# Sliding-window attention into an expert layer: five more of the stream's sums sessions in the turned form

## The chip, the cores and the metric

The kernel runs on one core of one Trainium2 chip. The metric is the device time of one execution in microseconds (us). Before the change three runs gave 301.45, 302.57 and 302.14 us; the median is 302.14 us.

## The reference

Attention with a window of 32 keys to each side, 8 batches of 8 heads, 576 positions, head width 64; then the heads side by side are the rows of x, 4608 tokens of 512, which go through a two-layer network with a SMELU between the layers.

```python
def _attn_ref(q, k, v):                      # 8, 8, 576, 64
    scores = scale * np.matmul(q, k.transpose(0, 1, 3, 2))
    mask = np.abs(pos[:, None] - pos[None, :]) <= 32
    scores = np.where(mask, scores, -1000000000.0)
    attn = np.exp(scores - np.max(scores, axis=-1, keepdims=True))
    attn = attn / (np.sum(attn, axis=-1, keepdims=True) + 1e-09)
    return np.matmul(attn, v)

def _moe_ref(x, w_in, w_out):                # 4608x512, 512x2048, 2048x512
    h = x @ w_in
    g = np.where(h >= 1, h, np.where(h <= -1, 0.0, (h + 1) ** 2 / 4))
    return g @ w_out
```

## The kernel before

Everything is in bf16 with f32 sums in PSUM, and one core does two kinds of work interleaved by hand: the attention, which makes x, and the two products of the network, which use it.

**Positions.** The main loop counts positions `a`. At each position it issues one projection `hp`: up to position 71 one token tile of 256 tokens and 256 of the 2048 hidden columns (line 653, eight matmuls), so eight positions to a tile; from 72 to 135 ("wide") 512 tokens and 128 columns (line 674, four matmuls), so sixteen positions to 512 tokens. The wide part begins with token 2304: positions 72 to 87 use tokens 2304 to 2815, positions 88 to 103 tokens 2816 to 3327. After the projection come its elementwise steps (line 692 on ScalarE, lines 698 and 700 on VectorE), then the attention work written down for this position, then a given number of matmuls of the second product (`op`, line 607 or 625), whose results leave through `osb` by a DMA on the sync engine's queue SP (line 615). PE takes its instructions in exactly this order.

**Sessions.** Batches 1 to 7 are one stream of 63 chunks of 64 keys. It is handled in turns, numbered from 0; from turn 5 on a turn has three chunks. At a position of the list below one turn's sums are made and the next turn's scores are begun; this is called session `k` here after the turn whose sums it makes.

```python
sl = [26.0, 29, 33, 36, 41, 45, 49, 53, 59, 66, 71, 74, 81, 87, 95, 99, 108, 111, 123]   # sessions 4, 5, 6, ...
```

So sessions 9 to 14 stand at positions 45, 49, 53, 59, 66 and 71. Session `k` (from 5 on) makes x for the 192 tokens that begin at 1120 + 192(k - 5): session 11 for 2272 to 2463, session 13 for 2656 to 2847, session 16 for 3232 to 3423. Hence positions 72 to 87 need session 13's x, and positions 88 to 103 session 16's. Position 64, the first of tile 8 (tokens 2048 to 2303), needs all of session 10's and the first 32 tokens of session 11's.

**Two forms of a session.** `stream_scores` (lines 282 to 294) makes the scores of a turn, their exponential `wt` and the band mask. Then:

- The plain form (`stream_sums`, line 410): v is the stationary side, 32 small matmuls; a column of ones against `rows` (the pairwise sum of two halves of `wt`, made by VectorE in lines 301 to 305) gives the denominators in 8 more matmuls; ScalarE turns them into reciprocals by Ln and Exp (lines 319 to 323); VectorE multiplies into `xT` (line 327), where x lies already the way the projection reads it.
- The turned form (`turned_sums`, line 346): `wt` is the stationary side and v with a column of ones moves, 48 small matmuls; the queries are then on the partitions and the denominator is one more column. VectorE makes the reciprocals (line 354) and two products into a tile `xn` (line 358); DMA transposes issued on SP (lines 364 and 367) write `xT`. `xn` has two buffers.

**Loads and the SP queue.** From batch 3 on, q and k of a batch come by GpSimd's DMA queue (POOL, line 106) into `qn` and `kn`, with v behind (line 116); each of the two has one buffer, so the loads of the next batch wait for the transposes of this one (a small copy on POOL, line 716, marks that). Once `qn` has landed, SP issues one DMA transpose `qT<-qn` (line 196), and one `kT<-kn` likewise; they stand in SP's order at positions 46 and 48 for batch 5, at 65 and 69 for batch 6, at 89 and 91 for batch 7. SP takes its instructions in order: one that waits holds all that stand behind it.

```python
xps: for b, positions in [[23, 24], [33, 34], [46, 48], [65, 69], [89, 91]]   # qT, kT of batches 3 to 7
```

Of the kernel before, what the change touches and what calls it, by code (L numbers as in the profile page):

```python
# [14 lines left out]
def kernel(  # L15
# [33 lines left out]
    LATE = 5  # L49
    SPLIT = range(20, 25)  # L50
    EARLY = 3, 4
    TURNED = range(14, 23)

    const = ctx.enter_context(tc.tile_pool(name="const", bufs=1))
    nat = ctx.enter_context(tc.tile_pool(name="nat", bufs=2))
# [208 lines left out]
    def stream_scores(k, eng, pool=ps_s):  # L264
# [30 lines left out]
        M = turn_of(k)  # L295
        if k in TURNED:
            return
# [9 lines left out]
    def turn_of(k):  # L307

        return next(m for s, e, m in STREAMS if s == turns[k][0])
# [61 lines left out]
    def stream_sums(k, pool=ps_n):  # L371

        if k in TURNED:
            return turned_sums(k, pool)
# [374 lines left out]
```

## Time and profile before

| | before |
|---|---|
| median of three runs | 302.14 us |
| the profiled execution | 301.69 us |
| its span, first to last instruction | 299.9 us |
| PE busy | 288.4 us, 96% |
| VectorE (DVE) busy | 230.3 us, 77% |
| ScalarE (ACT) busy | 188.9 us, 63% |
| DMA queue of POOL (q0), share of 16 engines | 91.6% |
| DMA queue of SP (q1), share of 16 engines | 30.3% |

The profile shows one execution. Times are microseconds from the start of the span. A row of a timeline gives start, duration, engine, source line, operation, output and input tiles and a count; an engine name with a q is that engine's instruction queue, where a DMA's duration is the time to issue it, not to finish it. "To landing" is the time from the issue to the data's arrival. Idle time of an engine that is not on the path costs nothing.

### The profile page before, as it was taken

The numbers are of one execution on the slowest core, as the hardware profiler recorded it, in microseconds if no ns is written. First come the engines' busy times: TensorE is split into PE (matmuls) and PEld (weight loads), VectorE is DVE, ScalarE is ACT, GpSimd is POOL, SyncE is SP. The second block draws the span as 40 slices with busy tenths as digits, with TensorE's granted clock in tenths as the row PEclk, the third lists the DMA queues.
The fourth block names the chain that finished last, engine by engine and source line by source line (L and its number), as shares of the span: only waits on it lengthen the run. The fifth ranks groups of instructions, "written<-read, shape, count | busy, mean of one in ns | idle before, by whom it ended". The sixth has DMA issues, their size and how long they took to land.

```text
span 299.9 us, 8061 instructions
## 1 busy us (share of the span) xinstructions
PE 288.4 (96%) x3349; PEld 177.9 (59%) x3380; DVE 230.3 (77%) x371; ACT 188.9 (63%) x345; POOL 79.5 (27%) x102
## 2 busy tenths in 40 slices
PE   8789999999999999999999999999999999999995
PEld 4468778876666666677654444444444444456544
DVE  3369887999999999889898889598878887546700
ACT  3678794777777666775875466565467446675301
POOL 8997450072190452091046000031000000000000
PEclk9999999999999999999999999999999999999999
DMA  9999999999999999999989971589212212100121
GB/s 153 182 189 201 179 189 156 180 160 146 183 161 136 198 192 158 197 140 158 136 124 123 179 91 42 113 148 135 65 35 63 61 37 62 37 35 36 39 103 70
DMA packets 146293, 37.45 MB, mean 125 GB/s; under 512 B 130129, under 2 KB 142673, under 8 KB 146257
## 3 DMA queue, kind: packets, MB, share of 16 engines
q0 software_dynamic: 103600, 18.06, 91.6%
q1 hardware_dynamic: 42512, 18.59, 30.3%
q8 instruction: 26, 0.43, 0.6%
q10 hardware_dynamic: 144, 0.29, 0.4%
q14 instruction: 11, 0.08, 0.1%
HBM read 36.70 MB, written 9.44 MB: 154 GB/s over the span
## 4 chain that ended last, share of the span: by engine, by line
PE 85%; DVE 4%; ACT 4%; issue 3%; DMA 2%; POOL 1%; POOLq 0%; ACTq 0%; DVEq 0%
PE op L607 35%; PE hp L653 20%; PE hp L674 18%; PE op L625 3%; PE bb L410 2%; DMA vn<-in_v_dram 2%; PE bb L282 2%; PE bb L346 2%; PE op L598 1%; DVE mx L698 1%; ACT rr L692 1%; POOL vn L116 1%; ACT rc L454 1%; PE tp L189 1%; DVE wt L294 1%
## 5 line engine op out<-in xcount | busy, mean ns | idle before, releaser
L692 ACT ACTIVATE rr<-hp 128x512 f32<-128x512 f32 x144 | 85.3, 595 | 80.2 <-PE hp L674 38.5
L607 PE MATMUL op<-w_out,gT 128*128 128x512 bf16 x471 | 120.0, 379 | 3.2 <-issue 3.0
L698 DVE TENSOR_TENSOR mx<-hp,rr 128x512 f32<-128x512 f32 x106 | 72.7, 686 | 16.2 <-ACT rr L692 15.3
L653 PE MATMUL hp<-xT,w_in 128*128 128x256 bf16 x640 | 82.5, 273 | 1.7 <-DMA w_in<-in_moe_w_in_dram 0.6
L700 DVE SCALAR_TENSOR_TENSOR gT<-rr,mx 128x512 bf16<-128x512 f32 x105 | 72.7, 692 | 3.6
L607 PEld LDWEIGHTS <-gT 128*128 128x128 bf16 x496 | 47.0, 98 | 47.6
L653 PEld LDWEIGHTS <-w_in 128*128 128x128 bf16 x640 | 61.5, 98 | 21.3 <-issue 3.2
L674 PE MATMUL hp<-xT,w_in 128*128 128x512 bf16 x252 | 64.5, 379 | 0.2
L674 PEld LDWEIGHTS <-w_in 128*128 128x128 bf16 x256 | 25.0, 98 | 30.3 <-issue 0.2
L696 DVE SCALAR_TENSOR_TENSOR gT<-hp,mx 128x512 bf16<-128x512 f32 x38 | 26.2, 689 | 17.4 <-ACT mx L695 15.3
L116 POOL DMA_DIRECT2D vn<-in_v_dram x32 | 27.6, 879 | 2.1 <-issue 2.1
L695 ACT ACTIVATE mx<-rr 128x512 f32<-128x512 f32 x38 | 23.9, 630 | 1.2
L716 POOL COPY gate<-kT 128x2 bf16<-128x2 bf16 x4 | 1.4, 345 | 87.9 <-DMA kT<-kn 87.9
L288 ACT ACTIVATE wt<-bb 128x1024 bf16<-128x1024 f32 (+2 forms) x23 | 22.1, 966 | 3.6 <-PE bb L282 2.8
L294 DVE TENSOR_TENSOR wt<-wt,band 128x1536 bf16<-128x1536 bf16 (+2 forms) x23 | 20.4, 888 | 4.3 <-ACT wt L291 2.8
L611 ACT COPY osb<-op 128x512 f32<-128x512 f32 x23 | 13.3, 577 | 11.3 <-PE op L607 11.3
L625 PE MATMUL op<-w_out,gT 128*128 128x256 bf16 x128 | 16.3, 273 | 0.0
L106 POOL DMA_DIRECT2D qn<-in_q_dram x12 | 14.8, 1250 | 4.1 <-DMA kT<-kn 3.7
L106 POOL DMA_DIRECT2D kn<-in_k_dram x12 | 14.8, 1260 | 0.2 <-issue 0.2
L625 PEld LDWEIGHTS <-gT 128*128 128x128 bf16 x128 | 12.5, 98 | 1.4
L327 DVE TENSOR_TENSOR xT<-bb,rc 128x768 bf16<-128x768 f32 (+4 forms) x16 | 11.9, 754 | 1.8 <-ACT rc L323 1.7
L291 ACT ACTIVATE wt<-sp 128x256 bf16<-128x256 f32 (+1 forms) x36 | 11.2, 368 | 0.0
(88 smaller groups left out, 198.4 us busy)
## 6 DMA issues: line engine op xcount, KB each, us to landing
out_dram<-osb SPq DMA_DIRECT2D x30, 256.0 KB, 2.7
vn<-in_v_dram POOLq DMA_DIRECT2D x32, 144.0 KB, 5.7
qn<-in_q_dram POOLq DMA_DIRECT2D x12, 288.0 KB, 9.3
kn<-in_k_dram POOLq DMA_DIRECT2D x12, 288.0 KB, 10.8
w_in<-in_moe_w_in_dram POOLq DMA_DIRECT2D x15, 128.0 KB, 4.9
out_dram<-osb SPq DMA_DIRECT2D x12, 128.0 KB, 1.9
w_out<-in_moe_w_out_dram POOLq DMA_DIRECT2D x4, 256.0 KB, 9.5
w_out<-in_moe_w_out_dram POOLq DMA_DIRECT2D x2, 512.0 KB, 12.0
```

What stands on the lines that cost most here:

```text
L106: nc.gpsimd.dma_start(out=x[:, :, h], in_=src[b, NY * h:NY * h + NY].rearrange("y s d -> (y s) d") .rearrange("(u p) d -> p u d", p=128))
L116: nc.gpsimd.dma_start(out=vn[b][64 * a:64 * a + 64, :, h, :D], in_=v[b, y:y + 2].rearrange("y s d -> (y s) d") .rearrange("(c r) d -> r c ...
L294: V.tensor_mul(x, x, band[:, :128].rearrange("p (m n j) -> p m n j", m=1, n=1).to_broadcast(list(x.shape)))
L607: nc.tensor.matmul(op[tt], gT[:, j, home(tt // 2), 128 * (tt % 2):128 * (tt % 2) + 128], w_out[:, j], start=j == 0, stop=j == 15)
L625: nc.tensor.matmul(o[:, tt], gT[:, j, p, 128 * tt:128 * tt + 128], w_out[:, j, 256 * half:256 * half + 256], start=not done, stop=len(done ...
L653: nc.tensor.matmul(hp[:, j], w_in[:, kk, 256 * f + 128 * j:256 * f + 128 * j + 128], xT[:, kk, r0:r0 + TB], start=first and n == 0, stop=l ...
L674: nc.tensor.matmul(hp.rearrange("p n t -> p (n t)"), w_in[:, kk, 128 * f:128 * f + 128], xT[:, kk, r0:r0 + 2 * TB], start=n == 0, stop=n == 3)
L692: A.activation(rr, hp, AF.Relu, scale=0.5, bias=0.5)
L695: A.activation(mx, rr, AF.Square)
L696: V.scalar_tensor_tensor(g, hp, 1.0, mx, op0=ALU.max, op1=ALU.min)
L698: V.tensor_max(mx, hp, rr)
L700: V.scalar_tensor_tensor(g, rr, 1.0, mx, op0=ALU.min, op1=ALU.mult)
```

## The change

One constant: which sessions use the turned form.

```diff
-    TURNED = range(14, 23)
+    TURNED = range(9, 23)
```

Sessions 9, 10, 11, 12 and 13 go from `stream_sums` to `turned_sums`; positions, loads, pools and everything else stay. The function that they call now, shortened (its end, `scale`, is queued for VectorE at the next position):

```python
    def turned_sums(k, pool=ps_n):
        bb = two_banks(pool)
        s, m, lo, hi = ranges[k]
        ...
        for part in (todo[:8], todo[8:]):
            for back in (1, 0):
                for g, e, n, y, h in part:
                    ...
                    for a in range(2):
                        nc.tensor.matmul(bb[HD[e], a, E * n:E * n + E], wt[HD[a], 2 * h + y, j:j + 64],
                                         vn[1 + c // NC][HD[a], NC * y + c % NC, h, :E],
                                         start=(a, e) not in seen, stop=True, skip_group_check=True)
        def scale():
            V.reciprocal(rs, x[:, :, :, D])
            xn = early.tile([128, 2, S], BF, name="xn", tag="kh", bufs=2).rearrange("p h s -> p (h s)")
            ...
                V.tensor_mul(p.rearrange("p (a n d) -> p a n d", a=2, d=D), x[:, :, n0:n1, :D],
                             rs[:, :, n0:n1].rearrange("p a (n e) -> p a n e", e=1).to_broadcast([128, 2, n1 - n0, D]))
            t0 = (S + lo) % RING
            cuts = (32, 64) if RING - t0 == 32 else ()
            for p0, p1 in zip((0, *cuts), (*cuts, 128)):
                r0 = (t0 + p0) % RING
                nc.sync.dma_start_transpose(out=xT[:, :, r0:r0 + p1 - p0], in_=parts[0][p0:p1])
            r0 = (t0 + 128) % RING
            for y in range(2):
                nc.sync.dma_start_transpose(out=xT[:, y::2, r0:r0 + 64], in_=parts[1][HD[y]])
```

In the built program, SP's order around the new transposes becomes (those of lines 364 and 367 are "x"; an output is one transfer of line 615): two outputs, **x of 9**, an output, qT and kT of batch 5, **x of 10**, an output, **x of 11** (five DMAs, since its tokens cross the end of the ring that `xT` is), two outputs, **x of 12**, an output, qT of batch 6, **x of 13**, an output, kT of batch 6, x of 14, and so on as before. Each of the other four has three DMAs, so 17 are added.

## The prediction

> **What bounds the kernel now.** I read the page first: busy times, then the chain that ended last, then the queues and DMA issues.
>
> ```profile
> span 299.9 us, 8061 instructions
> PE 288.4 (96%) x3349; PEld 177.9 (59%) x3380; DVE 230.3 (77%) x371; ACT 188.9 (63%) x345; POOL 79.5 (27%) x102
> ...
> DMA  9999999999999999999989971589212212100121
> ...
> PE 85%; DVE 4%; ACT 4%; issue 3%; DMA 2%; POOL 1%; POOLq 0%; ACTq 0%; DVEq 0%
> ...
> xT<-xn SPq DMA_TRANSPOSE x27, 3.4
> ```
>
> PE is the bound: 85% of the chain is PE's. PE works in program order, so the time changes only through PE work removed or through a wait put in front of a PE instruction. The DMA row says where a wait could come from: the engines are full until slice 20 (about 150 us), and sessions 9 to 13 lie inside that; of those turned so far only 14 and 15 meet such load.
>
> Next the stretch of the five sessions, in the sums by windows (PE, PEld, DVE, ACT, POOL busy):
>
> ```profile
> 102.00:112.00 10.00, 9.81 (x183) 7.04 (x184) 9.52 (x15) 6.86 (x15) 6.20 (x7) 1.00 1.49 189
> ...
> sum 60.00, PE 58.94 PEld 41.12 DVE 53.88 ACT 42.50 POOL 17.47; mean PE 9.82 PEld 6.85 DVE 8.98 ACT 7.08 POOL 2.91
> ```
>
> From 92 to 152 us PE is idle for 60.00 - 58.94 = 1.06 us. No relief of another engine can gain more than that here.
>
> **The PE work of a session.** PE's timeline: sessions 9, 12 and 13 (plain, L410), 14 and 15 (turned, L346), the projections of positions 56 and 64 (L653, counted on from the sessions, whose positions are known), and the first wide one (L674):
>
> ```profile
> 102.86 0.54 PE L410 MATMUL bb<-wt,vn 64*64 64x64 bf16 x32
> ...
> 124.96 1.04 PE L653 MATMUL hp<-xT,w_in 128*128 128x256 bf16 x8
> ...
> 130.49 0.54 PE L410 MATMUL bb<-wt,vn 64*64 64x64 bf16 x32
> ...
> 139.05 1.04 PE L653 MATMUL hp<-xT,w_in 128*128 128x256 bf16 x8
> ...
> 142.62 0.54 PE L410 MATMUL bb<-wt,vn 64*64 64x64 bf16 x32
> ...
> 143.80 1.24 PE L607 MATMUL op<-w_out,gT 128*128 128x512 bf16 x5 [0.16 <-issue]
> ...
> 151.98 0.68 PE L346 MATMUL bb<-vn,wt 64*64 64x65 bf16 x48
> ...
> 153.16 0.81 PE L607 MATMUL op<-w_out,gT 128*128 128x512 bf16 x3 [0.16 <-issue]
> 153.81 1.03 PE L674 MATMUL hp<-xT,w_in 128*128 128x512 bf16 x4
> ...
> 158.86 0.58 PE L346 MATMUL bb<-vn,wt 64*64 64x65 bf16 x48
> ...
> 159.91 0.38 PE L607 MATMUL op<-w_out,gT 128*128 128x512 bf16 x1 [0.16 <-issue]
> ```
>
> From the first small matmul to the next large one: plain (13) 143.80 - 142.62 = 1.18; turned 153.16 - 151.98 = 1.18 and 159.91 - 158.86 = 1.05. So a turned session saves 0 to 0.13 us of PE, the five together 0 to 0.65; I take 0.3, near the middle, as the two turned rows are one at each end.
>
> **VectorE and ScalarE.** VectorE loses the row sums (L301) and the product into xT (L327), and gets a reciprocal (L354) and two products (L358):
>
> ```profile
> L327 DVE TENSOR_TENSOR xT<-bb,rc 128x768 bf16<-128x768 f32 (+4 forms) x16 | 11.9, 754 | 1.8 <-ACT rc L323 1.7
> L358 DVE TENSOR_TENSOR xn<-bb,rs 128x512 bf16<-128x512 f32 (+1 forms) x18 | 9.2, 553 | 0.3
> L301 DVE TENSOR_TENSOR rows<-wt 128x768 bf16<-128x768 bf16 (+1 forms) x11 | 5.6, 510 | 0.4
> L354 DVE RECIPROCAL rs<-bb 128x12 f32<-128x12 f32 x9 | 2.0, 225 | 0.0
> ```
>
> That is 0.754 + 0.510 = 1.26 out, 0.225 + 2 x 0.553 = 1.33 in: nothing. The Ln and Exp on ScalarE go, and with them VectorE's short waits for them. PE hides both: it waits for neither, by the 1.06 us above. I cost them at nothing.
>
> **The DMA transposes, and who waits.** The five sessions add 17 DMAs to SP, on transfers that share the engines with the loads. SP's timeline, then POOL's around the loads of batches 6 and 7:
>
> ```profile
> 117.50 3.78 SPq L196 DMA_TRANSPOSE qT<-qn  x1
> ...
> 142.39 4.41 SPq L196 DMA_TRANSPOSE qT<-qn  x1
> ...
> 148.53 3.26 SPq L196 DMA_TRANSPOSE kT<-kn  x1
> 156.39 1.19 SPq L364 DMA_TRANSPOSE xT<-xn  x1
> 157.67 2.48 SPq L367 DMA_TRANSPOSE xT<-xn  x2
> ```
>
> ```profile
> SPq L196 <- DMA qn<-in_q_dram: 88.9, 7, 47.5
> ```
>
> ```profile
> 127.39 0.73 POOL L716 COPY gate<-kT 128x2 bf16<-128x2 bf16 x1 [13.33 <-DMA kT<-kn]
> ```
>
> The second fence is SP's waits: SP's qT transposes wait for qn, whose loads come behind the batch before's kT through the gate on POOL. It is one serial chain: kT of batch 5, gate, loads of batch 6, qT of batch 6 at 142.39. Before the change only outputs stood behind that wait. Now x of 13 stands right behind qT of batch 6, and x of 10 behind batch 5's; whoever waits for x is PE.
>
> Deadlines: position 72 at 153.81 needs x of 13; position 64 at 139.05 needs x of 10 and the head of x of 11. x of 9 is needed at position 56, 22 us after its session (124.96 - 102.86), and x of 12 at 72, 23 us after (153.81 - 130.49): projections hide both.
>
> How long x takes is in the turned sessions' landings, with loads running (156 to 168 us) and without (205 to 256 us), line 364:
>
> ```profile
> DMA to landing us min/median/max: 6.3/7.1/8.0
> ```
>
> ```profile
> DMA to landing us min/median/max: 2.4/2.4/4.3
> ```
>
> What x costs the loads is in the DMA issues of 128 to 138 us, where no x is on the queue, and of 154 to 164 us, where two sets are:
>
> ```profile
> qn<-in_q_dram POOLq DMA_DIRECT2D x2, 288.0 KB, 9.6
> kn<-in_k_dram POOLq DMA_DIRECT2D x2, 288.0 KB, 11.3
> ```
>
> ```profile
> qn<-in_q_dram POOLq DMA_DIRECT2D x2, 288.0 KB, 9.2
> kn<-in_k_dram POOLq DMA_DIRECT2D x2, 288.0 KB, 14.3
> ```
>
> Two sets make kn land 3.0 us later and qn not at all: 1.5 us a set at the end of the loads, 0 for the part loaded first. The upper bound is the engines' whole time for a set, a third of a qT or kT by bytes, whose landings (line 196, 90 to 160 us) were:
>
> ```profile
> DMA to landing us min/median/max: 4.9/5.9/8.4
> ```
>
> So at most 8.4 / 3 = 2.8 us a set. The Trainium skill, "DMA: Bandwidth & Descriptors", section "Issuing engines are not separate DMA queues", speaks against the change: DMAs of different engines run on the same 16 engines and interleave, so a second queue saves issue time alone. By that rule a set would cost its full engine time, the upper bound; qn's rows say less, kn's half of it.
>
> *Delay of qT of batch 6.* In its chain are x of 9 (during batch 5's loads) and, during batch 6's, x of 10 (its tail), 11 and 12: about 3.5 sets. Bounds 0 and 3.5 x 2.8 = 9.8 us. The chain passes through kn and kT of batch 5, so the 1.5 applies to x of 9; for qn of batch 6 the truth is between 0 and 1.5 a set. I take 1.3 a set, near the upper of these because outputs too now fall into that load: 4.5 us.
>
> *x of 13.* Its first DMA can go when its VectorE work is done, by session 14's delay 142.62 + (156.39 - 151.98) = 147.03, and when SP has issued qT, 142.39 + 4.41 = 146.80: together, with no delay. Plus 4.5 it goes at 151.5; the last of the three starts 2.5 later (157.67 + 1.24 - 156.39) and lands 3.4 after that, the median of all 27 x transposes, between 2.4 and 8.0, nearer the unloaded end because the loads of batch 6 are almost in. That is 157.4, against 153.81: PE waits **3.6 us** in front of position 72. With the bounds: no delay and 2.4 gives 151.95, in time by 1.9; 9.8 and 8.0 gives 167.4, late by 13.5.
>
> *x of 10 and 11.* Batch 5's kT follows its qT (117.50 + 3.78 = 121.3), with x of 9's price of 1.5 to 2.8 at about 123.3; its issue takes some 3.3 us, x of 10's three DMAs 3.7, so the head of 11 goes by about 131, behind an output. Landing in 8.0 it is there at 139.0: just in time for 139.05. A wait here comes off the next one. Cost nothing; if late, it is part of the 3.6.
>
> *What is late next.* kT of batch 6 goes behind x of 13, at 151.5 + 3.7 = 155.2 instead of 148.53, and batch 7's loads, which wait for it, come some 7 us later too. They then meet x of 16:
>
> ```profile
> 176.79 3.57 SPq L367 DMA_TRANSPOSE xT<-xn  x2
> ```
>
> ```profile
> 183.59 1.03 PE L674 MATMUL hp<-xT,w_in 128*128 128x512 bf16 x4
> ```
>
> Its last DMA starts at 176.79 + 3.57 - 1.24 = 179.1 (an issue is 2.48 / 2 = 1.24) and position 88 needs it at 183.59. Landing in 2.4 leaves 2.1 us, in 8.0 it is late by 3.5. Loads reach there only in part; I take 0.5. Later sessions meet no loads. The outputs queued behind have `osb`'s three buffers.
>
> *A wait and the clock.* The granted clock is 1.00 in the windows above. At the very start PE was slow, in its timeline, against the end, in the chain in order of time:
>
> ```profile
> 1.20 4.88 PE L506 MATMUL z<-gT 128*128 128x512 bf16 x11 [1.20 <-DVE gT L138]
> ```
>
> ```profile
> 281.35 5.83 PE op L607 x27
> ```
>
> 4.88 / 11 = 0.44 us a matmul there against 5.83 / 27 = 0.22 later: half speed. If a wait brought that back for as long, it would cost 2.4 us. The Trainium skill, "TensorE: Matmul & The Clock Gate", section "What's actually happening", says an idle window of about 3.4 us does so; by that rule a wait of 3.6 lies at its edge.
>
> **Sum.** 301.69 of the profiled execution (1.8 of it outside the span) - 0.3 + 3.6 + 0.5 = 305.5 us. The median shown is 302.14, 0.45 above that execution, inside its own spread, so I add nothing.
>
> **The rivals.**
>
> *In time: not slower.* The loads give way less than I think. From 154 us on qn landed in 9.2 with two sets beside it, 9.6 without: for it a set cost nothing. If the delay of qT stays under about 0.9 us with 3.4 to land (1.9 with 2.4), x of 13 arrives before 153.81 and only PE's saving is left: 301.69 - 0.3 = 301.4, 301.0 with all of it. Against it: kn's 3.0 us, and x's own 7.1. It decides at that 1 to 2 us of delay.
>
> *Late and cold.* As forecast, and PE comes back at half speed for a stretch: 305.5 + 2.4 = 307.9; with a full-price delay (2 us a set, 7.0 in all, and so 2.5 more) 310.4. For: PE's idle time of 1.06 us in 60 shows no wait of this size, so no row tells what follows one. Against: it needs a wait longer than forecast, or a poor phase.
>
> *Late by both bounds.* The engines give each set its whole time and x lands as under load: over 310, up to 315.
>
> **How the numbers follow.** Late, forecast: 0.55. Late and cold: 0.17. In time or late by under 2 us: 0.23. By both bounds: 0.05. The range goes from the in-time case, 301.3, to late and cold, 310. About 0.5%, 1.5 us either way of 302.14, is what a measurement of this kernel can tell from no change. Faster by that would need 300.6: more than all PE's saving, 0.03. Same: the in-time case and waits of up to 2 us, 0.2. Slower: 0.77. The forecast case's own range is 303.7 to 308.
>
> **What would show it.** Right: PE idle of 2 to 7 us just before the first L674, ended by a DMA `xT<-xn`; qT of batch 6 issued at 145 to 149; L346 x672 in all, and no L319 to L323 from 100 to 150 us; each of the five session stretches 1.05 to 1.18. Cold: PEclk below 9 after that wait. Wrong: qT of batch 6 still near 142.4 and no wait at position 72; or a wait elsewhere, at position 64 or on VectorE for an `xn` buffer, which I hold to be free in time.

## The result, and the profile after

The changed kernel takes 311.97 us (median of six runs, 308.06 to 314.2) against 301.87 of the kernel before (also six): slower by a ratio of 1.0284, 95% interval 1.0253 to 1.0315. Every ratio here leaves out runs that lie over 1.5% above the fastest of the same kernel, of this set 313.93 and 314.2 us, while the medians are of all runs. The profiled execution took 312.66 us, its span is 310.9. A second set of five runs gave 310.31 and a ratio of 1.0269 (1.0247 to 1.0291).

The page of the changed kernel first: span and busy times, the slices of PE, its granted clock and the DMA engines, then two groups.

```profile
span 310.9 us, 8162 instructions
PE 292.8 (94%) x3389; PEld 178.7 (57%) x3420; DVE 229.3 (74%) x374; ACT 181.7 (58%) x325; POOL 80.2 (26%) x102
...
PE   8789999999999999959969999999999999999995
...
PEclk9999999999999999995997999999999999999999
DMA  9999999999999999999997999199311201101021
...
L653 PE MATMUL hp<-xT,w_in 128*128 128x256 bf16 x640 | 84.7, 277 | 5.9 <-DVE mx L698 4.3
...
L358 DVE TENSOR_TENSOR xn<-bb,rs 128x512 bf16<-128x512 f32 (+1 forms) x28 | 14.3, 553 | 5.3 <-DMA xT<-xn 4.8
```

The span grew by 11.0 us, PE's busy time by 4.4 (288.4 to 292.8). PE's row has two dents, the eighteenth and the twenty-first slice, and just behind each the granted clock falls: PE stood still twice and then ran slowly. The group of L358 names a wait that the prediction had ruled out: VectorE waited 4.8 us, once, for a DMA transpose.

PE's timeline of the changed kernel, from session 12 (130.40) on:

```profile
130.40 0.58 PE L346 MATMUL bb<-vn,wt 64*64 64x65 bf16 x48
...
140.39 1.87 PE L653 MATMUL hp<-xT,w_in 128*128 128x256 bf16 x8 [4.02 <-DVE mx L698]
...
149.49 0.58 PE L346 MATMUL bb<-vn,wt 64*64 64x65 bf16 x48
...
158.72 0.68 PE L346 MATMUL bb<-vn,wt 64*64 64x65 bf16 x48
...
163.10 1.61 PE L674 MATMUL hp<-xT,w_in 128*128 128x512 bf16 x4 [2.40 <-DVE xn L358]
```

In square brackets is PE's idle time before the row. Session 8 began at 94.96 (before: 94.65, a difference from the start of the span), session 12 at 130.40 (before: 130.49): three turned sessions (9 to 11) have won 0.40 us, 0.13 each, and nothing is lost yet. Session 13 comes 6.87 us late (142.62 before), session 14 6.74 (151.98 before), session 15 at 169.86 instead of 158.86, 11.0 late; from there the two kernels run alike. So there are two losses: around position 62 6.87 + 0.09 + the 0.13 that session 12 won, 7.1 us, and around position 72 11.0 - 6.74 = 4.3 us. Of the first 4.02 is waiting, of the second 2.40; the rest, 3.1 and 1.9, is slow running. The sums by windows, with the granted clock as third figure from the end, show it:

```profile
120.00:136.00 16.00, 15.69 (x172) 10.58 (x174) 11.89 (x20) 9.80 (x18) 3.59 (x5) 1.00 1.48 144
136.00:140.00 4.00, 0.38 (x2) 0.10 (x1) 1.28 (x3) 0.55 (x2) 4.00 (x5) 0.94 1.96 173
140.00:147.00 7.00, 6.38 (x28) 4.00 (x29) 4.40 (x7) 1.45 (x3) 1.11 (x1) 0.55 2.90 102
147.00:160.00 13.00, 12.68 (x222) 9.13 (x223) 11.00 (x18) 7.70 (x14) 0.00 (x0) 1.00 1.83 175
160.00:164.00 4.00, 1.60 (x6) 0.42 (x5) 3.17 (x6) 1.24 (x3) 0.00 (x0) 0.93 0.29 58
164.00:168.00 4.00, 4.00 (x13) 1.55 (x12) 1.38 (x2) 1.94 (x4) 0.00 (x0) 0.64 1.18 199
```

Behind the first wait the clock is 0.55 over 7 us, behind the second 0.64 over 4; the eight matmuls of one projection at 140.39 took 1.87 us where they take 1.04 at full clock.

What made PE wait is on VectorE's, ScalarE's and SP's timelines of the changed kernel:

```profile
133.69 0.23 DVE L354 RECIPROCAL rs<-bb 128x12 f32<-128x12 f32 x1
138.72 1.02 DVE L358 TENSOR_TENSOR xn<-bb,rs 128x512 bf16<-128x512 f32 x2 [4.81 <-DMA xT<-xn]
```

```profile
139.66 0.59 ACT L611 COPY osb<-op 128x512 f32<-128x512 f32 x1 [3.45 <-DMA out_dram<-osb]
```

```profile
107.39 1.19 SPq L364 DMA_TRANSPOSE xT<-xn  x1
108.67 2.52 SPq L367 DMA_TRANSPOSE xT<-xn  x2
123.11 4.08 SPq L196 DMA_TRANSPOSE qT<-qn  x1
127.35 2.73 SPq L196 DMA_TRANSPOSE kT<-kn  x1
130.19 1.22 SPq L364 DMA_TRANSPOSE xT<-xn  x1
131.51 3.40 SPq L367 DMA_TRANSPOSE xT<-xn  x2
...
151.84 6.39 SPq L196 DMA_TRANSPOSE qT<-qn  x1
158.32 1.22 SPq L364 DMA_TRANSPOSE xT<-xn  x1
159.67 2.88 SPq L367 DMA_TRANSPOSE xT<-xn  x2
```

x of 9 (107.39) runs beside batch 5's loads; qT of batch 5 goes at 123.11 instead of 117.50, and x of 10 behind it only at 130.19. Session 12 needs the `xn` buffer that x of 10 is read from, so VectorE stands still from 133.9 to 138.7 with all its elementwise work behind it, and PE runs out of free `hp` tiles: the first wait. ScalarE stood still until 139.66 as well, for an output that SP issued behind x of 10 (at 135.01); this trace alone does not separate the two. qT of batch 6 then goes at 151.84 instead of 142.39, and x of 13, right behind it, at 158.32: PE waits for it at position 72, the second wait. (The profile names VectorE there, a product for session 14 that ended at 163.0; the second DMA of x of 13 landed then too, 3.3 us after its issue at 159.67, and position 72 needs it.)

The second set's profiled execution of the same kernel (312.38 us) lost about as much, but by other waits. PE's timeline and SP's:

```profile
137.67 1.03 PE L653 MATMUL hp<-xT,w_in 128*128 128x256 bf16 x8 [1.16 <-DVE mx L698]
...
142.00 1.05 PE L653 MATMUL hp<-xT,w_in 128*128 128x256 bf16 x8 [1.53 <-DMA xT<-xn]
...
161.96 1.87 PE L674 MATMUL hp<-xT,w_in 128*128 128x512 bf16 x4 [5.11 <-DMA xT<-xn]
```

```profile
120.65 4.19 SPq L196 DMA_TRANSPOSE qT<-qn  x1
...
147.20 7.51 SPq L196 DMA_TRANSPOSE qT<-qn  x1
154.80 1.23 SPq L364 DMA_TRANSPOSE xT<-xn  x1
```

Here PE waited 7.80 us in all, most of it at position 72, and only the last wait had half speed behind it. qT of batch 6 was less late, but SP took 7.51 us to issue it.

### The profile page after: what moved, and what is told of

Same layout as the page of the kernel before. It is cut to its first block, busy times and chain, and to the rows that moved or that the text cites. A ratio compares the mean times of both kernels' runs of the same rounds, so it can differ in the third digit from the quotient of the medians.

```text
span 310.9 us, 8162 instructions
## 1 busy us (share of the span) xinstructions
PE 292.8 (94%) x3389; PEld 178.7 (57%) x3420; DVE 229.3 (74%) x374; ACT 181.7 (58%) x325; POOL 80.2 (26%) x102
## 5 line engine op out<-in xcount | busy, mean ns | idle before, releaser
L653 PE MATMUL hp<-xT,w_in 128*128 128x256 bf16 x640 | 84.7, 277 | 5.9 <-DVE mx L698 4.3
L653 PEld LDWEIGHTS <-w_in 128*128 128x128 bf16 x640 | 62.4, 99 | 26.9 <-issue 8.4
L674 PE MATMUL hp<-xT,w_in 128*128 128x512 bf16 x252 | 65.8, 385 | 2.6 <-DVE xn L358 2.4
L674 PEld LDWEIGHTS <-w_in 128*128 128x128 bf16 x256 | 25.2, 99 | 33.7 <-issue 4.3
L358 DVE TENSOR_TENSOR xn<-bb,rs 128x512 bf16<-128x512 f32 (+1 forms) x28 | 14.3, 553 | 5.3 <-DMA xT<-xn 4.8
```

Source lines behind the costliest of these rows:

```text
L653: nc.tensor.matmul(hp[:, j], w_in[:, kk, 256 * f + 128 * j:256 * f + 128 * j + 128], xT[:, kk, r0:r0 + TB], start=first and n == 0, stop=l ...
L674: nc.tensor.matmul(hp.rearrange("p n t -> p (n t)"), w_in[:, kk, 128 * f:128 * f + 128], xT[:, kk, r0:r0 + 2 * TB], start=n == 0, stop=n == 3)
```

## The experiments

**Fewer sessions turned.** Two kernels:

```diff
-    TURNED = range(9, 23)
+    TURNED = range(13, 23)     # t13
+    TURNED = range(12, 23)     # t12
```

> One session (13) turned instead of five. Theory, that the time is lost because x of the turned sessions shares the DMA engines with the loads of batches 5 and 6: here x meets next to none of them, qT of batch 6 stays near 142.4 us, x of 13 lands at 152 to 154 us against position 72 at 153.8, and the time is 301.0 to 302.5 us. Rival, that the SP order alone (x of 13 behind qT) costs the second wait: a PE wait of about 2 us stays in front of position 72, 304 us.

> Sessions 12 and 13 turned. Theory (loads and x share the engines): one set beside the loads of batch 6 delays its qT by some 4 to 5 us, x of 13 lands at 156 to 158 us, PE waits 2 to 4 us at position 72: 303.5 to 307 us. Rival (the xn buffers alone): no buffer is short here, 301.5 us.

Session 13 alone: 301.79 us, ratio 0.9999 (0.9985 to 1.0013). Sessions 12 and 13: 303.78 us, ratio 1.0057 (1.0035 to 1.0079). SP's timeline of the first, then of the second:

```profile
142.71 4.32 SPq L196 DMA_TRANSPOSE qT<-qn  x1
147.28 1.93 SPq L364 DMA_TRANSPOSE xT<-xn  x1
```

```profile
134.85 1.34 SPq L364 DMA_TRANSPOSE xT<-xn  x1
136.29 2.53 SPq L367 DMA_TRANSPOSE xT<-xn  x2
145.19 4.06 SPq L196 DMA_TRANSPOSE qT<-qn  x1
```

One set, x of 12, beside the loads of batch 6 moves its qT from 142.71 to 145.19: 2.5 us. The delay is less than the 4 to 5 us expected; the time is within what was expected. PE then waits 1.35 us within position 72, in the second kernel's timeline:

```profile
155.65 0.60 PE L674 MATMUL hp<-xT,w_in 128*128 128x512 bf16 x2 [1.35 <-DMA xT<-xn]
```

Standing behind qT costs nothing when qT is on time, which rules the order alone out, and the xn buffers alone too, since 12 and 13 find theirs free.

**The turned form without its transfers.** In `scale`, for sessions 9 to 13 (the part of `xT` that then stays unwritten is zeroed once at the start):

```diff
+            if k < 14:
+                return
             t0 = (S + lo) % RING
```

> Five sessions turned up to xn, but their 17 DMA transposes left out (x of those tokens stays at what stood there), so the turned form without its transfers. Theory: PE's small saving is all that is left, 301.0 to 301.9 us, no wait above 0.3 us between 90 and 170 us, qT of batch 6 near 142.4. Rival (something else of the turned form costs, on PE or VectorE): 303 us or more.

301.38 us, ratio 0.9984 (0.9965 to 1.0003); qT of batch 6 at 141.52. So no cost of the turned form on PE, VectorE or ScalarE shows, and what it brought without its transfers is about half a microsecond, with an interval that includes none.

**The transfers without the turned form.** The kernel before, with its plain sums, and behind each of the five sessions three transposes that nobody reads (15 in all instead of 17; they write one spare tile, so SP waited up to 2.6 us for the set before):

```diff
+                nc.sync.dma_start_transpose(out=spill[:, :, :128], in_=gift[:, :512])
+                for y in range(2):
+                    nc.sync.dma_start_transpose(out=spill[:, y::2, 128:], in_=gift[HD[y], 512:])
```

> The kernel before, sessions 9 to 13 in the plain form, but with DMA transposes of the same sizes issued on SP behind each of these sessions, from a tile of zeros into a spare tile that nobody reads: the transfers without anyone waiting for them. Theory: they delay qT of batch 6 by 4 to 9 us (146 to 151 us), but its scores come long after, so PE does not notice: 301.5 to 302.7 us. Rival (the load on the engines itself stops PE, through loads, outputs or qT): 305 us or more.

305.05 us (303.28 to 307.74), ratio 1.0118 (1.0079 to 1.0157): my theory had said no loss, and the time is that of the rival. qT of batch 6 came at 151.72. The kernel's waits tell where, and the time to landing of the first transpose of x of session 16, issued between 176 and 178 us:

```profile
PE hp L687 <- DVE rs L357: 1.8, 1, 1.8
```

```profile
DMA to landing us min/median/max: 9.0/9.0/9.0
```

PE waited once, 1.82 us, in front of position 88: the loads of batch 7 were late too, and now x of session 16, turned already in the kernel before, ran among them and landed 9.0 us after its issue at 176.59, at 185.6, with position 88 starting at 185.69 (the profile names VectorE). This is the next late thing that the prediction had priced at 0.5. To see whether that is all:

```diff
-    TURNED = range(14, 23)
+    TURNED = (14, 15, *range(17, 23))      # and the transfers that nobody reads
```

> As the run with transposes that nobody reads, but session 16 in the plain form, so that position 88 no longer waits for a transpose of its x. That run had one PE wait, 1.82 us in front of position 88, where the first transpose of x of 16 landed at 185.6 us among the late loads of batch 7. Theory (delayed loads cost nothing except where PE waits for a transpose among them): the wait goes, 301.7 to 302.8 us. Rival (the transfers cost PE in another way): 304 us or more, with waits elsewhere.

302.80 us (302.08 to 304.95), ratio 1.0040 (1.0022 to 1.0058): most of the loss is gone, not all, and the median lies at the upper end of what was expected. The profiled execution, at 304.68 one of the longest, still waits at position 88, for the last transpose of x of session 15, in its PE timeline:

```profile
187.23 0.59 PE L687 MATMUL hp<-xT,w_in 128*128 128x512 bf16 x2 [1.83 <-DMA xT<-xn]
```

So most of what delayed loads cost PE goes with projections that wait for a DMA transpose among them: in these two traces no other wait of PE from 100 us on exceeds 0.3 us. That the loads cost nothing besides is not shown, as 0.4% remains and one trace with a wait does not account for the other runs.

**Four buffers for xn.**

```diff
-                     ... tag="kh", bufs=2)
+                     ... tag="kh", bufs=4)
```

(The buffers are shared by name with an early tile of k, whose line gets the same number.)

> All five sessions turned, xn with four buffers instead of two, so VectorE no longer waits for x of 10 to have left. Theory (late x, whatever waits for it first): the wait of 4.0 us near 136 us goes, but position 64 now waits for the head of x of 11 and position 72 for x of 13, which still lands near 160 us or later: 309 to 313 us, as changed. Rival (the two buffers are the cause of the first loss of 6.9 us): 304 to 306 us.

310.24 us, ratio 1.0271 (1.0237 to 1.0304): as slow as with two. VectorE's wait is gone; in PE's timeline the waits have moved to positions 64 and 72:

```profile
141.31 1.05 PE L653 MATMUL hp<-xT,w_in 128*128 128x256 bf16 x8 [2.50 <-DMA xT<-xn]
...
160.27 0.80 PE L674 MATMUL hp<-xT,w_in 128*128 128x512 bf16 x2 [4.15 <-DMA xT<-xn]
```

PE lost as much without the shortage of buffers: it was the first place where late x showed, not the cause. ScalarE still waited for an output, 1.8 us, and PE's timeline has no wait there. The x of 13 landed at 159.5 to 161.4 us.

**The order on SP.** With the four buffers, the qT of batch 6 behind x of 13; then also qT and kT of batch 5 behind x of 10 and 11:

```diff
-  [[23, 24], [33, 34], [46, 48], [65, 69], [89, 91]]
+  [[23, 24], [33, 34], [46, 48], [67, 69], [89, 91]]     # xn4_q67
+  [[23, 24], [33, 34], [54, 55], [67, 69], [89, 91]]     # order
```

> Five sessions turned, xn with four buffers, and SP's qT of batch 6 moved from position 65 to 67, behind x of 13. Theory A (x of 13 is late because it stands behind a qT that waits for delayed loads): x of 13 goes at 147 to 152 us, the wait at position 64 of about 2.5 us stays, that at 72 shrinks to 0 to 2: 304 to 307 us. Theory B (the engines' load alone decides, the order does not matter): x lands as late as with four buffers alone, 309 to 311 us.

> As the one before, and qT and kT of batch 5 moved from positions 46 and 48 to 54 and 55, behind x of 10 and of 11. Theory A (standing behind a waiting qT makes x late): no wait at position 64 any more; loads of batch 6 start some 7 us later and now run beside x of 12 and 13, which may leave 0 to 4 us at position 72: 301.5 to 306 us. Theory B (the engines' load alone): 308 us or more.

305.60 us, ratio 1.0113 (1.0050 to 1.0176), and 305.01 us, ratio 1.0083 (1.0054 to 1.0112). Both lie in theory A's range, and over half of the loss, by the ratios 58% and 69%, goes with where x stands in SP's order. With both moves position 64 waits no more, and position 72 less:

```profile
155.45 0.59 PE L674 MATMUL hp<-xT,w_in 128*128 128x512 bf16 x2 [1.96 <-DMA xT<-xn]
156.54 1.01 PE L674 MATMUL hp<-xT,w_in 128*128 128x512 bf16 x2 [0.50 <-DMA xT<-xn]
```

What is left is x of 13 itself among the loads of batch 6: issued at 146.45, its pieces landed 7.4 to 7.8 us after their issue. So both halves count: x lands late among the loads, and the wait for qT makes it start late.

**The clock behind a wait.** The changed kernel with matmuls whose results nobody uses, in front of the two projections that waited:

```diff
+        if a in (62, 72):
+            z = two_banks(ps_s)
+            for _ in range({62: 18, 72: 11}[a]):
+                nc.tensor.matmul(z[:, 0], w_in[:, 0, :128], w_in[:, 0, :512], start=True, stop=True)
```

> The changed kernel with dummy matmuls (results unused) in front of the projections at positions 62 (18) and 72 (11), where PE waited 4.02 and 2.40 us: PE is busy in these waits instead of idle. Theory (part of the loss is the clock at half speed behind a wait, 10.2 us of it in the changed kernel's trace): the clock stays at 1.00 and the waits remain, 305.5 to 308 us, against 312.0. Rival (the waits are all of it, the clock record costs nothing): 311 to 313 us.

309.27 us, ratio 1.0229 (1.0184 to 1.0275), between what the theory and the rival had expected. Its PE timeline shows the 18 matmuls in the place of the wait, and the projection behind them at full speed:

```profile
136.12 4.05 PE L670 MATMUL bb<-w_in 128*128 128x512 bf16 x18
140.01 1.04 PE L653 MATMUL hp<-xT,w_in 128*128 128x256 bf16 x8
```

The profiled span is 305.9 us against 310.9, with the clock at 1.00, but this is the fastest of four runs against one of the longer of six. And VectorE went on at 135.70 here, as at 136.00 in the second set's execution, where PE waited 1.16 us, so by estimate the 18 dummies, 4.05 us, were longer than the wait that they stood in for. Beside the changed kernel on one chip, five rounds each:

> The changed kernel again, on the same chip as the next one. Both theories: 310 to 313 us, with the clock between 0.98 and 0.995 and the time rising as the clock falls.

> The kernel with dummy matmuls in the waits again, beside the changed kernel on the same chip. Theory (half speed behind a wait is part of the loss): faster than the changed kernel by 2 to 5 us, clock 1.00. Rival (it costs nothing): the same within 1 us.

310.31 us (309.27 to 312.38) and 309.33 (307.59 to 311.76): 1.0 us apart, as the rival had said (within 1 us), with ratios of 1.0269 (1.0247 to 1.0291) and 1.0245 (1.0209 to 1.0281) whose intervals overlap. The dummies are of fixed length: where a run's wait is shorter they cost PE themselves, and where it is longer, PE stands idle again (one of the six had a clock of 0.994). That half speed can follow a wait and what it costs PE there is shown by the trace (1.87 for 1.04); how much a median would gain without it is not settled by these runs.

## Why the prediction was wrong

The direction was right, and the wait that was forecast came: PE in front of the first wide projection, for x of 13 behind a late qT of batch 6. The size was not: 305.5 forecast, at most 310.0, and 311.97 measured. In the profiled execution the larger part of the waiting, 4.02 of 6.42 us, came from a deadline that the prediction had called kept, and 5.0 us more from the clock. The time is that of the rival "late by both bounds" (over 310, chance 0.05), but only half its mechanism is there: the sets cost more than their bound, while x of 13 landed 2.8 to 4.3 us after its issue, near the 3.4 forecast, in this execution. By its steps:

- *PE's saving, 0.3 us; VectorE and ScalarE at nothing.* Held, and at its upper end: 0.13 us a session in the trace, 0.65 if all five give that, and a ratio of 0.9984, about 0.5 us, without the transfers.
- *Price of a set, 1.3 us, at most 2.8.* This is the term that failed first. x of 9 moved qT of batch 5 by 5.6 us in the profiled execution (117.50 to 123.11). In the six traces with x of 9 beside these loads this qT went at 118.6 to 123.1, in the four without any set there at 117.5 to 118.8; in four of the six it came over 2.8 us later than before, past the bound. x of 12 alone cost 2.5. The bound was a third of one transpose's landing, which supposes that the engines lose only the time that the set would take by itself. The DMA queues in 110 to 118 us, where these loads run, of the kernel before and then of the changed one, in packets, MB and share of 16 engines:

```profile
q0 software_dynamic: 8015, 1.02, 201.8%
q1 hardware_dynamic: 144, 0.26, 8.7%
```

```profile
q0 software_dynamic: 4851, 0.62, 291.9%
q1 hardware_dynamic: 879, 0.26, 48.5%
```

  With 735 more packets of SP's queue, the loads moved 3164 fewer: 39% less in 8 us. Why the two cost each other so much stays open. The rule of the Trainium skill that the prediction weighed ("DMA: Bandwidth & Descriptors", "Issuing engines are not separate DMA queues": all queues share the 16 engines) pointed the right way, but its reading as full engine time, 2.8 us a set, was still too little in four of six traces. The rows on which I took 1.3, two sets beside batch 7's loads, were one sample of a cost that varies from execution to execution.
- *Delay of qT of batch 6, 4.5 us.* It was 9.45 in the profiled execution (142.39 to 151.84), just inside the upper bound of 9.8. In the second set's it was 4.8 (147.20), as forecast, and the time was no better: the prediction had let SP issue this transpose in 4.41 us, as before, and it took 6.39 in the first and 7.51 in the second, with x of 13 behind it, and in the second x landed 4.7 to 6.5 us after its issue. PE began position 72 at 163.10 and 161.96, where x was forecast for 157.4. So the step that failed in both is when x of 13 is there; which of its terms was off, the delay or the issue and the landing, changed between executions.
- *xn buffers "free in time"; x of 10 and 11 at nothing.* Wrong, and by the same error: with qT of batch 5 at 123.11, x of 10 left its buffer only at 138.7 and session 12 wanted it at 133.9. The prediction gives no sum for this deadline, and that of position 64, which it did work out, came out "just in time" with no slack: with four buffers PE waited 2.50 us there, in the second set's execution 1.53. The buffers of `osb`, also counted as enough, ran out once too (3.45 us on ScalarE). The shortage of xn buffers did not add a loss of its own, as four buffers show; it took its share earlier. Without the first wait x of 13 would have made PE wait up to 163.10 - 153.81 = 9.3 us at position 72, an estimate that leaves x of 13 where it was, against 6.4 of waiting in all.
- *The clock.* The case "late and cold" had 0.17 and one price of 2.4 us. It was the rule: the mean granted clock was 0.982 to 0.994 in all eleven runs of the changed kernel and 0.998 to 1.000 in those of the kernel before, and in the profiled execution half speed behind both waits cost 3.1 and 1.9 us. The Trainium skill's figure ("TensorE: Matmul & The Clock Gate", "What's actually happening": an idle window of about 3.4 us) bears on it; the first wait of 4.02 exceeds it, the second, 2.40, does not, yet the clock fell there too. The length of the wait alone does not decide: 1.99 us with qT of batch 6 moved brought half speed, the 2.50 us with four buffers did not (the projection behind it took 1.05), nor did the 1.82 and 1.83 with transfers that nobody reads and the 1.35 of sessions 12 and 13.
- *What is late next, 0.5 us.* In the changed kernel it did not show, as PE had fallen 11 us behind by then; with the transfers alone it was 1.82 us of waiting in the profiled execution, and the median was 1.2% longer.

The sum as it came out in the profiled execution: 301.69 + 0.31 from the start - 0.65 saved + 4.02 + 2.40 waited + 3.1 + 1.9 at half speed gives 312.8 against 312.66. The last two were got as remainders of the two losses, so the sum checks the bookkeeping, not the causes.

No version here beats the kernel before: with session 13 alone the time is the same, and with no transfers at all the gain is 0.16%, with an interval that includes none.

## What to carry to other kernels

When work moves from an engine to the DMA queues, compare the stretch it lands in with one that already carries the same mix, and check every deadline, the reuse of a buffer among them, against the upper price and not the likely one: here late transposes broke the deadline with the least slack first, and removing that one only handed the wait to the next. A transfer issued behind another that waits in the same queue inherits that wait; moving it ahead won back more than adding buffers did. And a wait of PE costs more than its length when the clock drops behind it. One trace shows one execution: where queues race, look at a second one before naming the term that failed.

## What the runs showed of the hardware

- DMA transposes and small loads on the same engines slowed each other: from 110 to 118 us the loads moved 4851 packets instead of 8015 while SP's queue moved 735 packets more, though no more bytes (0.26 MB), and x landed 8.3 to 8.5 us (medians, 107 to 150 us) after its issue, against 2.4 with no loads beside it.
- Half speed came in stretches of 3.4 us or twice that. In these traces the granted clock changes only at times that lie whole multiples of 3.41 us apart (139.54, 146.37, 163.44 and 166.85 in the changed kernel). Counted in such stretches, PE was idle for 1.99 to 3.40 of the 3.41 us before each of the six drops behind a wait, and for at most 1.75 in any stretch at full clock with no drop behind it. The wait of 2.50 with four buffers fell into two stretches, 1.23 and 1.27, which is why its length alone did not tell.
- The same program spread over 308.06 to 314.2 us, where the kernel before stayed within 301.36 to 303.42 over all its sets here. In the changed kernel the time hangs on when transfers of different queues land, and that moved by several us between executions: qT of batch 6 went at 151.84 in one and at 147.20 in the other.
